# V ahead of the state-space scan in the first head block, the weights of one deferred segment mean asked for sooner, and two deferred means put later in stage 2

## The chip, the cores and the metric

The kernel runs on one core of a Trainium2 chip. The metric is the device time of one execution in microseconds (us). The kernel before takes 1317.5 us (median of 4 runs, 1315.62 to 1318.15). A program on one core has no other core to compare its clock with, so a run counts as slow only if it is more than 1.5% above the fastest of the same kernel.

Names of engines: PE is TensorE's matmul stream, DVE is VectorE, ACT is ScalarE, POOL is GpSimd, SP is SyncE, whose queue issues nearly all DMA transfers here (SPq in the trace). A *tag* (P, R, S, O; psP and so on in the trace) names a set of buffers for matmul results.

## The reference, cut to what matters

Two independent layers share one launch, and their outputs are laid side by side.

```python
# A: a diagonal state-space layer (S5), x is 2048 x 1024
Bu = einsum('bld,pd->blp', x, B_bar)
for t in range(L):
    h = Lam_bar * h + Bu[:, t]
y = 2 * einsum('blp,dp->bld', hs, C).real + x * Dskip

# B: attention with 8 memory rows, over segments of 32 tokens, 32 heads of 128
for s in range(64):
    h = concat(mem, x_segment)            # 8 + 32 rows
    q, k, v = h Wq, h Wk, h Wv
    o = softmax(mask(q k^T * scale)) v
    o = o Wo;  mem = o[:8];  out_s = o[8:]
```

The kernel does not walk B's 64 segments one after the other. It first guesses each segment's memory rows from the mean of the segment before (mean of x, times Wv, times Wo), does all segments in parallel, and checks the guess at the end. The *segment means* in this text are the products of these means of x with Wv, one for each of eight head blocks of four heads.

## The kernel before

The parts that matter are the first phase, in which A's scan and B's V share the engines, and its seam with the second phase (stage 2).

For each of 8 blocks of A's state (`pc`) and each of 4 token blocks (`tb`), `stage1` runs 16 matmuls on A's transposed x and hands the result to VectorE, which does the complex scan: about twenty operations for each token block. Between these, `v_x` runs 32 matmuls of V for the same token block of B, and ScalarE evicts them.

```python
    def v_x(self, hb, w):                        # V = x Wv, four 512-token groups
        for q in range(4):
            st = self.wl.tile([128, 4, 512], BF16, name="b_vst", bufs=2)
            for i in range(4):
                t = 4 * q + i
                p = k.ps("P")                    # 3 buffers
                for c in range(KC):
                    k.PE.matmul(p[:], self.xe[:, c, t * 128:(t + 1) * 128], w[:, c, :], ...)
                k.copy("s", st[:, i, :], p[:])   # ScalarE
                ...                              # store to DRAM after each group

    def og(self, hb, w):                         # one head block's segment means
        p = k.ps("R")                            # 1 buffer
        for h in range(4):
            for c in range(KC):
                k.PE.matmul(p[:, h * NSEG:(h + 1) * NSEG], w[:, c, h * 128:(h + 1) * 128], self.xbar[:, c, :], ...)
        k.V.tensor_copy(self.ogT[:, hb * 4:(hb + 1) * 4, :], p[...])
```

Before the means can be formed, VectorE must have summed x over each segment (`sum_x`, 18 reductions, most of 1.1 us here). It is done with that in block 2; the means of blocks 2 to 7 then follow inside the loop, and those of blocks 0 and 1 are *deferred* to stage 2, where their weights are loaded a second time:

```python
            a.load_x(0)
            b.load_x(0)
            ...
            for pc in range(PC):
                v = b.v_x(pc, wv)
                for tb in range(NB):
                    if pc == 0 and tb + 1 < NB:
                        a.load_x(tb + 1)
                    a.stage1(pc, tb)
                    if pc == 0:
                        b.load_x(tb + 1)
                    if tb == 1 and pc + 1 < PC:
                        nxt = b.load_wv(pc + 1)          # b_wv has two buffers
                    ...
                    for _ in range(4):
                        next(v, None)
                    if pc >= 1:
                        next(sx, None), next(sx, None)   # two sums over x
                if pc == 2:
                    b.fin_xbar(p1)
                if pc >= 2:
                    b.og(pc, wv)
        ...
            g = b.guess(p2)              # means times Wo, pieces of 2 MB (b_wog)
            s2 = a.stage2(p2)            # 32 halves of 16 matmuls each
            wv = [b.load_wv(0), b.load_wv(1)]
            for i, _ in enumerate(s2):
                if i in (1, 2):
                    b.og(i - 1, wv[i - 1])
                if i > 2 and i % 2 == 1:
                    next(g, None)
                if i == 16:
                    b.load_wqk(0)        # q and k weights of the next phase
```

Inside stage 2, each half ends with a VectorE addition into `a_ot` (two buffers), and each pair with a store of that tile. Stores, loads of the next x (`a_xn`), of the scan's states (`a_hl`) and of `b_wog` all go through the one queue of SP:

```python
                    V.tensor_tensor(ot[:, hs], py[:], xd[:, hs], ALU.add)
                    yield
                k.SP.dma_start(self.out[0, t0:t0 + 128, 0:D], ot[:])
                if 4 * tb + tt + 3 < TT:
                    load_xn(4 * tb + tt + 3, k.SP)
```

The order of instructions on each engine is set when the program is built, by a scheduling pass, and is not the order of the source. `keep_in_program_order` and `issue_after` are the builder's means to pin it.

## Time and profile before

| | before |
|---|---|
| time, median | 1317.5 us |
| span of the profiled run | 1314.3 us |
| PE busy | 1265.9 us (96%) |
| first large matmul | 14.53 us |
| first segment mean (end of the VectorE-bound part) | 148.30 us |
| stage 2 begins | 377.76 us |

The page of the kernel before, part 1 (busy time of each engine) and two rows of part 2 (busy tenths in 40 slices of the span, about 33 us each):

```profile
PE 1265.9 (96%) x7807; PEld 658.7 (50%) x7874; DVE 673.4 (51%) x1500; ACT 426.6 (32%) x1135; POOL 211.0 (16%) x291
PE   5999999999969999999999999999999989999997
DVE  6999998988821214555555555545555530001000
```

PE is the limit over the whole, with holes in the first slice and in the twelfth, which is the seam before stage 2. VectorE's 51% is an average: it is at 8 or 9 tenths in slices 2 to 11 and low afterwards. The windows view splits it at the first mean (columns: window, length, then busy time and instruction count of PE, PEld, DVE, ACT, POOL, granted clock, DMA share, GB/s):

```profile
18.00:148.30 130.30, 123.19 (x557) 55.08 (x566) 130.03 (x253) 48.51 (x85) 3.88 (x27) 1.00 0.76 185
148.30:361.00 212.70, 211.66 (x1130) 99.33 (x1149) 193.34 (x366) 75.39 (x134) 8.51 (x10) 1.00 0.40 123
```

Up to 148 us, VectorE is busy for 130.03 of 130.30 us and PE for only 123.19; from there on PE is busy for 211.66 of 212.70 us and VectorE for only 193.34.

The chain of waits of PE (what it waited for, total us, times, longest), then that of VectorE in the first 149 us:

```profile
PE psR L398 <- DMA b_wv<-in_B_Wv_dram: 8.1, 1, 8.1
PE psR L135 <- DMA a_r_119<-in_A_log_dt_dram: 6.8, 1, 6.8
PE psS L225 <- DMA a_xT<-in_A_x_dram: 6.6, 1, 6.6
PE psR L398 <- DVE b_ogT L399: 4.5, 1, 4.5
PE psP L380 <- ACT b_vst L62: 3.6, 6, 1.1
PE psP L380 <- DMA b_xe<-in_B_x_dram: 2.9, 2, 2.4
```

```profile
DVE b_xsum L353 <- DMA b_xe<-in_B_x_dram: 5.8, 1, 5.8
DVE a_raw L137 <- PE psR L135: 4.6, 1, 4.6
DVE ones L75 <- PEq L931: 0.9, 1, 0.9
```

L135 is the small transpose of A's parameters, from which VectorE makes the scan's tables. PE does nothing large before 14.5 us. VectorE idles 4.6 us for the parameters and 5.8 us for B's first x; these and two small waits sum to 11.5 us, and after 18 us it never stops.

The first large matmul and then the seam, in the timeline of PE (start, duration, instruction group, in brackets the idle time before and its releaser):

```profile
14.53 3.18 PE L225 MATMUL psS<-a_xT,a_bt_178 128*128 128x512 bf16 x8 [6.63 <-DMA a_xT<-in_A_x_dram]
...
360.17 1.10 PE L398 MATMUL psR<-b_xbar,b_wv 128*128 128x64 bf16 x32
365.73 1.87 PE L398 MATMUL psR<-b_xbar,b_wv 128*128 128x64 bf16 x32 [4.46 <-DVE b_ogT L399]
375.65 1.89 PE L398 MATMUL psR<-b_xbar,b_wv 128*128 128x64 bf16 x32 [8.06 <-DMA b_wv<-in_B_Wv_dram]
377.76 1.85 PE L289 MATMUL psO<-t_105,a_hl_3615 128*128 128x512 bf16 x5 [0.22 <-issue]
```

The mean of block 7 is followed by that of block 0, which waits until VectorE has copied block 7's out of the only buffer of tag R, then by that of block 1, which waits for its weights. Only then does stage 2 (L289) begin, although the source puts both means behind halves of stage 2. VectorE is late with that copy partly because one of its scans took 4.61 us at 355.99 us, where others take 1.28, while GpSimd ran two multiplications of 2.14 and 2.12 us from 355.30 on:

```profile
355.30 2.14 POOL L282 TENSOR_TENSOR a_xd<-a_xn_3609,a_dB 128x1024 f32<-128x1024 bf16 x1
...
355.99 4.61 DVE L237 TENSOR_TENSOR_SCAN a_wr<-a_rr,a_nx,a_wr 128x512 f32<-128x512 f32 x1
```

The Trainium skill, "SBUF — State Buffer", "SBUF: two separate sides", tells of a port pair for which a VectorE operation with two SBUF inputs and a GpSimd operation that reads SBUF exclude each other; this trace agrees at this one place, with 4.61 us for the scan.

The 8 matmuls at 14.53 take 3.18 us and a later group of 8 takes 1.89: a cold start. The Trainium skill, "TensorE: Matmul & The Clock Gate", Part 1, gives half the clock after an idle window of about 3.4 us; here the first matmuls after such a pause lie 0.43 us apart and later ones 0.216, which agrees.

### The profile page before, as it was taken

What the parts mean: (1) busy time and instruction counts of PE and PEld (TensorE: products, weight loads), DVE (VectorE), ACT (ScalarE), POOL (GpSimd) and SP (SyncE); (2) the same over time, 40 slices, a digit from 0 to 9 for tenths busy, and PEclk for the clock granted to TensorE, in tenths of its full rate; (3) what the DMA queues carried; (4) which work ended last, traced back from release to release, by engine and by line L of the source; (5) the groups of instructions that cost most, each with busy time, mean ns of one, the idle gap of its engine ahead of it and who ended that gap; (6) DMA issues with size and microseconds to landing.
All of it is one profiled execution on the core that took longest, in us unless ns stands there. A gap on an engine that the chain in (4) does not pass through costs nothing. (4 is left out here: it accounts for less than half of the span.)

```text
span 1314.3 us, 20077 instructions
## 1 busy us (share of the span) xinstructions
PE 1265.9 (96%) x7807; PEld 658.7 (50%) x7874; DVE 673.4 (51%) x1500; ACT 426.6 (32%) x1135; POOL 211.0 (16%) x291
## 2 busy tenths in 40 slices
PE   5999999999969999999999999999999989999997
PEld 2444444444435545555555555555555544444443
DVE  6999998988821214555555555545555530001000
ACT  3433333333200001554544454444545540001000
POOL 5000000000112221222222222222222220000000
PEclk9999999999979999999999999999999989999999
DMA  9983443344399519323343434333333470403000
GB/s 248 246 199 116 120 131 100 107 129 144 120 258 321 167 48 255 91 83 110 99 133 99 133 99 133 99 89 95 91 88 81 136 241 17 136 24 121 16 25 18
DMA packets 230843, 163.15 MB, mean 124 GB/s; under 512 B 74880, under 2 KB 214768, under 8 KB 230744
## 3 DMA queue, kind: packets, MB, share of 16 engines
q1 hardware_dynamic: 229272, 158.18, 42.1%
q0 software_dynamic: 1408, 3.61, 0.8%
q8 instruction: 63, 1.03, 0.3%
q14 instruction: 36, 0.29, 0.1%
q10 hardware_dynamic: 64, 0.02, 0.0%
HBM read 95.72 MB, written 49.30 MB: 110 GB/s over the span
## 5 line engine op out<-in xcount | busy, mean ns | idle before, releaser
L380 PE MATMUL psP<-b_wv,b_xe 128*128 128x512 bf16 x1021 | 227.4, 379 | 6.6 <-ACT b_vst L62 3.6
L516 ACT ACTIVATE b_e<-psS 99x396 bf16<-99x396 f32 x176 | 88.2, 501 | 417.9 <-PE psS L513 415.7
L519 POOL TENSOR_TENSOR b_m<-b_e,maskB 99x396 bf16<-99x396 bf16 x160 | 139.4, 871 | 351.6 <-ACT b_e L516 351.6
L539 DVE TENSOR_TENSOR b_ot<-psO,b_r 128x384 bf16<-128x384 f32 x176 | 98.1, 557 | 188.6 <-ACT b_r L533 169.8
L380 PEld LDWEIGHTS <-b_xe 128*128 128x128 bf16 x1024 | 99.9, 98 | 129.3 <-issue 5.9
L604 PEld LDWEIGHTS <-b_ol 128*128 128x128 bf16 x896 | 87.8, 98 | 106.5 <-issue 1.9
L64 DVE CAST b_ost<-psP 128x512 bf16<-128x512 f32 x16 | 11.1, 692 | 193.5 <-PE psP L604 193.5
L62 ACT ACTIVATE b_vst<-psP 128x512 bf16<-128x512 f32 x128 | 73.6, 586 | 109.5 <-PE psP L380 90.0
L604 PE MATMUL psP<-t_4702,b_ol 128*128 128x512 bf16 x438 | 99.7, 382 | 0.7 <-issue 0.2
L604 PE MATMUL psP<-wo_12093,b_ol 128*128 128x512 bf16 x438 | 98.8, 379 | 0.5
L533 ACT ACTIVATE b_r<-b_ln 128x396 f32<-128x396 f32 x176 | 94.0, 534 | 5.4
L532 ACT ACTIVATE b_ln<-psR 128x396 f32<-128x396 f32 x176 | 86.9, 494 | 0.0
L62 ACT ACTIVATE b_ost<-psP 128x512 bf16<-128x512 f32 x16 | 9.6, 597 | 211.4 <-PE psP L604 198.2
L291 DVE TENSOR_TENSOR a_ot<-psO,a_xd 128x512 bf16<-128x512 f32 x32 | 22.1, 692 | 94.9 <-PE psO L289 87.5
L64 DVE CAST b_k_4707<-psP 128x480 bf16<-128x480 f32 (+2 forms) x96 | 48.7, 529 | 30.6 <-PE psP L489 30.0
L528 PE MATMUL psR<-b_m,ones 99*128 99x396 bf16 x176 | 59.2, 337 | 3.1 <-POOL b_m L519 2.2
L537 PE MATMUL psO<-b_m,b_v 99*128 99x99 bf16 x704 | 61.5, 209 | 0.0
L64 DVE CAST b_k_4715<-psP 128x480 bf16<-128x480 f32 (+2 forms) x96 | 48.7, 528 | 21.3 <-PE psP L489 21.3
L64 DVE CAST b_q_4703<-psP 128x480 bf16<-128x480 f32 (+2 forms) x96 | 48.7, 528 | 17.5 <-PE psP L489 17.5
L537 PEld LDWEIGHTS <-b_v 99*128 99x128 bf16 x704 | 50.6, 98 | 13.3 <-DVE b_omT L542 0.6
L64 DVE CAST b_q_4711<-psP 128x480 bf16<-128x480 f32 (+2 forms) x96 | 48.6, 527 | 12.5 <-PE psP L489 12.5
L248 ACT ACTIVATE a_gr<-a_wr 128x512 bf16<-128x512 f32 x32 | 20.2, 630 | 68.7 <-DVE a_wr L237 68.7
(722 smaller groups left out, 1950.9 us busy)
## 6 DMA issues: line engine op xcount, KB each, us to landing
b_wv<-in_B_Wv_dram SPq DMA_DIRECT2D x16, 1024.0 KB
b_wog<-in_B_Wo_dram SPq DMA_DIRECT2D x4, 2048.0 KB
out_dram<-a_ot SPq DMA_DIRECT2D x16, 256.0 KB
t_4702<-in_B_Wo_dram SPq DMA_DIRECT2D x1, 4096.0 KB
b_ol<-b_os_90 SPq DMA_DIRECT2D x4, 1024.0 KB
b_ol<-b_os_91 SPq DMA_DIRECT2D x4, 1024.0 KB
b_ol<-b_os_92 SPq DMA_DIRECT2D x4, 1024.0 KB
wo_12093<-in_B_Wo_dram SPq DMA_DIRECT2D x1, 4096.0 KB
```

Of the source, the lines that this page charges most:

```text
L62: self.S.activation(out, in_, ACT.Copy)
L64: self.V.tensor_copy(out, in_)
L291: V.tensor_tensor(ot[:, hs], py[:], xd[:, hs], ALU.add)
L380: k.PE.matmul(p[:], self.xe[:, c, t * 128:(t + 1) * 128], w[:, c, :], start=(c == 0), stop=(c == KC - 1))
L516: k.S.activation(e[:], s[0:GW], ACT.Exp, scale=float(E) ** -0.5, accum_out=self.accE[0:GW, i:i + 1])
L519: k.G.tensor_tensor(m[:], e[:], mask[0:GW, :, :].unsqueeze(2).to_broadcast([GW, 2, 2, GW]), ALU.mult)
L528: PE.matmul(sm[:, 0:W4], k.ones[0:GW, :], mf, start=True, stop=True)
L532: k.S.activation(ln[:], sm[:, 0:W4], ACT.Ln)
L533: k.S.activation(r[:].rearrange("p a b q -> p (a b q)"), ln[:], ACT.Exp, scale=-1.0, accum_out=self.accR[:, i:i + 1])
L537: PE.matmul(o[:, gg, hh, :], vt[:, 2 * u + gg, hh * 128:(hh + 1) * 128], m[:, gg, hh, :], start=True, stop=True)
L539: V.tensor_tensor(ot[:, :, 2 * u * GX:(2 * u + 2) * GX].rearrange("p h (g n) -> p g h n", n=GX), o[:, :, :, 0:GX], r[:, :, :, 0:GX], ALU.mult)
L604: PE.matmul(p[:], lhs, self.wo[half][:, h, :], start=(h == 0), stop=(h == H - 1))
```

## The change

The intent has two parts. *Start*: V needs only B's x and Wv, so in head block 0 V of each 512 tokens is put ahead of the scan of its token block, and B's first x comes in four pieces of 128 tokens, so that PE can start at the first of them. *Middle*: the weights of block 0's deferred mean are fetched at `pc == 7` instead of at the seam, and both means are moved behind the third and fifth half of stage 2, into tag P, which has three buffers.

```diff
     def load_x(self, q):
+        for t, c, n in self.chunks(q):
+            step = 128 if q == 0 else n
+            for o in range(0, n, step):
+                self.k.SP.dma_start_transpose(self.xe[:, :, c + o:c + o + step], self.x[0][t + o:t + o + step, :])
 ... (chunks of 512, 512, 512, 384 and twice 64 tokens in place of four of 480 and twice 64)
-    def og(self, hb, w):
-        p = k.ps("R")
+    def og(self, hb, w, tag="R"):
+        p = k.ps(tag)
 ...
             wv = b.load_wv(0)
-            b.wl.tile([128, 4, 512], BF16, name="b_vst", bufs=2)
+            b.load_x(0)
             a.params(p1, p1)
 ...
             a.load_x(0)
-            b.load_x(0)
 ...
-                    if pc == 0 and tb + 1 < NB:
-                        a.load_x(tb + 1)
+                    if pc == 0:
+                        for _ in range(4):
+                            next(v, None)
+                        if tb + 1 < NB:
+                            b.load_x(tb + 1)
+                            a.load_x(tb + 1)
                     a.stage1(pc, tb)
-                    if pc == 0:
-                        b.load_x(tb + 1)
-                    if tb == 1 and pc + 1 < PC:
-                        nxt = b.load_wv(pc + 1)
+                    if tb == 1:
+                        nxt = b.load_wv((pc + 1) % PC)
 ...
-                    for _ in range(4):
-                        next(v, None)
+                    if pc > 0:
+                        for _ in range(4):
+                            next(v, None)
 ...
-            wv = [b.load_wv(0), b.load_wv(1)]
+            wv = [wv, b.load_wv(1)]
             for i, _ in enumerate(s2):
-                if i in (1, 2):
-                    b.og(i - 1, wv[i - 1])
-                if i > 2 and i % 2 == 1:
+                if i in (2, 4):
+                    b.og(i // 2 - 1, wv[i // 2 - 1], "P")
+                if i > 4 and i % 2 == 1:
                     next(g, None)
```

More of the change, by code (lines that the diff above doesn't have):

```diff
@@ L337, in load_x, with chunks @@
     def load_x(self, q):
-        k = self.k
-        if q < 4:
-            parts = [(64 + 480 * q, 480 * q, 480)]
-        else:
-            parts = [(0, XMAIN, 64), (T - 64, T - 64, 64)]
-        for t, c, n in parts:
-            k.SP.dma_start_transpose(self.xe[:, :, c:c + n], self.x[0][t:t + n, :])
+        for t, c, n in self.chunks(q):
+            step = 128 if q == 0 else n
+            for o in range(0, n, step):
+                self.k.SP.dma_start_transpose(self.xe[:, :, c + o:c + o + step], self.x[0][t + o:t + o + step, :])
+    @staticmethod
+    def chunks(q):
+        if q < 3:
+            return [(64 + 512 * q, 512 * q, 512)]
+        return [(64 + 1536, 1536, 384), (0, XMAIN, 64), (T - 64, T - 64, 64)]
     def sum_x(self):
         k = self.k
-        for t, c, n in [(64 + 480 * q, 480 * q, 480) for q in range(4)] + [(0, XMAIN, 64), (T - 64, T - 64, 64)]:
+        for t, c, n in sum((self.chunks(q) for q in range(4)), []):
             m = 2 if n > 64 else KC
```

## The prediction

> **What bounds the kernel now.** TensorE (PE): 1265.9 of 1314.3 us busy (page, part 1); some 48 us are idle: 14.5 until its first large matmul; 2.9 for pieces of B's x and 3.6 for ScalarE's evictions of psP, up to 148 us; and between the last scan block and stage 2 (361 to 377 us) 4.5 for VectorE's copy of the previous segment mean (one buffer of tag R), then 8.1 for the weights of head block 1 (chain of waits, timeline). After such pauses the first six or seven matmuls are 0.43 us apart, later ones 0.216: the half clock of the Trainium skill, "TensorE: Matmul & The Clock Gate", Part 1 (some 3.4 us after idling); this trace agrees with about 3 us, a loss of about 1.5 us each time.
>
> VectorE (DVE) is the second limit: from 18.0 to 148 us it is busy 129.7 of 130.0 us (windows), and PE's waits for evictions come from it. Before that it idles 5.8 us, until B's first x lands at 18.0.
>
> **What the change does.** PE's work is the same.
>
> 1. Start. B's x comes first, in 128-token pieces. A 512-token transpose takes about 4.5 us of the queue, so a piece should take 1.1 to 1.3. The DMA share is above 1 from 0 to 80 us at about 250 GB/s. From the trace's landing times (1.25 MB by 8.0 us, 2.5 MB by 14.5, then about 0.26 MB per us) I estimate: Wv and the first piece at 8 us, A's first x at 18 to 19. PE starts at 8, runs 32 V matmuls (about 8.5 us with the cold start), waits 2 us, and scans from 18.5 instead of 14.5. VectorE's first product comes no sooner, but its former idle time takes the first sums over x (1.2 us each) and parameters. So of PE's 6.5 us VectorE allows its idle 5.8 less some delay: I expect 3 to 6 us left at 148 us, kept afterwards since PE binds from there (101.5 of 102 us busy to 250).
>
> 2. Middle. The source moves the means behind the third and fifth half of stage 2, into tag P. If they run there, waits of 12.7 us and a cold restart of about 2 us go: about 14 us, less some DMA pressure (share 1.07 from 370 to 430 us). But an engine's order is not the source's: before, too, the source put both means behind stage-2 halves, and the trace has both ahead of the first. Nor is the fetch sooner: block 0's weights were already issued at 321 us, and block 1's (367 us) still wait for the last mean to free their buffer. If both means are again hoisted, PE waits for the same landing at 375.6 us, and nothing is gained. I give hoisting 0.65.
>
> **Sum.** Hoisted: about 1312. Not hoisted: about 1298. I say 1309 us, range 1296 to 1317. Faster by over 2% (below 1291) needs more than both gains: 0.04; within 2%: 0.95; slower: 0.01.
>
> **What would show it.** Timeline of PE: first large matmul (L380) near 8 us, first L225 at 18 to 19; VectorE's idle time before 18 us mostly gone; the first mean (148.3 us before) 3 to 6 us earlier. Middle: whether L289 follows the mean of block 7 directly or after two more, and whether the wait of 8 us for b_wv is gone or has grown to about 13.
>
> **What would make it wrong.** Pieces of x or stores queued between them hold up A's x by over 5 us, so the start becomes a loss; stage 2, begun sooner, outruns its loads; or the means are not hoisted and the start gives 6 us or more (1295).

## The result, and the profile after

The kernel after takes 1314.55 us (median of 4 runs, 1313.92 to 1316.48) against 1317.5 us. Ratios in this text are the mean time of one kernel's fast runs over that of the other's of the same rounds, so they are not quite the ratios of the medians quoted. Here the ratio is 0.9982, with a 95% interval of 0.9965 to 1.0. That is about 2.4 us (0.18% of 1317) and at the edge of what the runs can tell from nothing. The prediction was 1309 us, a gain of 8.5 us, more than three times as much.

The page after, part 1, and the waits of PE:

```profile
PE 1267.0 (97%) x7808; PEld 658.2 (50%) x7874; DVE 673.7 (51%) x1500; ACT 427.1 (33%) x1135; POOL 211.4 (16%) x291
```

```profile
PE psP L383 <- DMA b_xe<-in_B_x_dram: 11.2, 4, 8.0
PE psP L401 <- DMA b_wv<-in_B_Wv_dram: 10.0, 1, 10.0
PE psP L383 <- ACT b_vst L62: 4.7, 6, 2.9
```

The waits for A's parameters and for `b_ogT` are gone from PE's list, and the wait for `b_wv` has grown from 8.1 to 10.0 us.

*The start did what was intended, on PE.* PE's timeline after:

```profile
8.02 1.89 PE L383 MATMUL psP<-b_wv,b_xe 128*128 128x512 bf16 x4 [8.02 <-DMA b_xe<-in_B_x_dram]
9.85 0.20 PE L135 MATMUL psR<-ident,a_r_122 24*128 24x24 bf16 x1
...
19.88 1.89 PE L225 MATMUL psS<-a_xT,a_bt_181 128*128 128x512 bf16 x8 [2.27 <-DMA a_xT<-in_A_x_dram]
...
146.68 1.89 PE L383 MATMUL psP<-b_wv,b_xe 128*128 128x512 bf16 x8 [2.88 <-ACT b_vst L62]
148.40 1.10 PE L401 MATMUL psR<-b_xbar,b_wv 128*128 128x64 bf16 x32
```

The first large matmul begins at 8.02 us instead of 14.53. At the first mean all of that is gone: 148.40 us against 148.30. PE had the V products done sooner, and then waited longer. The wait of 2.88 us at 146.68 shows for what. It names ScalarE, which was to evict the V product; ScalarE's own timeline shows that it stood at another instruction, one that needed VectorE (the second line is the eviction that PE waited for):

```profile
145.42 0.72 ACT L193 ACTIVATE a_tabc_1760<-a_k_1764,hpb 128x513 f32<-128x513 f32 x1 [3.56 <-DVE a_wi L232]
146.05 0.58 ACT L62 ACTIVATE b_vst<-psP 128x512 bf16<-128x512 f32 x1
```

So the limit up to 148 us is VectorE's list of work, and what counts is VectorE's idle time before it. Its waits after, up to 149 us:

```profile
DVE a_raw L137 <- PE psR L135: 7.6, 1, 7.6
DVE b_xsum L356 <- DMA b_xe<-in_B_x_dram: 1.7, 2, 1.2
DVE a_wr L229 <- PE psS L225: 1.1, 2, 0.9
DVE ones L75 <- PEq L936: 0.9, 1, 0.9
```

The wait for B's x fell from 5.8 to 1.7 us, as intended. But the parameters' transpose (L135) now stands behind four V matmuls, which start only when x has landed at 8.02 us, so the wait for it rose from 4.6 to 7.6; and 1.1 us of waits for the scan's own input came in, because A's x now lands at 19.88 us instead of 14.53. With one more of 0.2 the total is 11.5 us, the same as before.

*The middle.* PE's timeline at the seam:

```profile
360.26 1.10 PE L401 MATMUL psR<-b_xbar,b_wv 128*128 128x64 bf16 x32
361.90 1.09 PE L401 MATMUL psP<-b_xbar,b_wv 128*128 128x64 bf16 x32 [0.54 <-ACT b_vst L62]
372.99 1.89 PE L401 MATMUL psP<-b_xbar,b_wv 128*128 128x64 bf16 x32 [9.99 <-DMA b_wv<-in_B_Wv_dram]
374.69 0.61 PE L289 MATMUL psO<-t_105,a_hl_3617 128*128 128x512 bf16 x1
```

Both means were hoisted ahead of stage 2's first half again. Tag P removed the wait of 4.5 us before block 0's mean, and the wait for block 1's weights took it over. They landed 2.66 us sooner (372.99 against 375.65), though their load was issued at the same moment (367.07 against 366.98 us, SP's timeline). That is about the whole of the gain; what may be behind it stands under e12.

### The profile page after: what moved, and what is told of

It is laid out like the page before. It is cut to its first block, busy times and chain, and to the rows that moved or that the text cites. A ratio compares the mean times of both kernels' runs of the same rounds, so it can differ in the third digit from the quotient of the medians.

```text
span 1312.2 us, 20083 instructions
## 1 busy us (share of the span) xinstructions
PE 1267.0 (97%) x7808; PEld 658.2 (50%) x7874; DVE 673.7 (51%) x1500; ACT 427.1 (33%) x1135; POOL 211.4 (16%) x291
## 5 line engine op out<-in xcount | busy, mean ns | idle before, releaser
L383 PE MATMUL psP<-b_wv,b_xe 128*128 128x512 bf16 x1024 | 229.8, 381 | 16.0 <-DMA b_xe<-in_B_x_dram 11.2
L383 PEld LDWEIGHTS <-b_xe 128*128 128x128 bf16 x1024 | 100.0, 98 | 139.3 <-DMA b_xe<-in_B_x_dram 12.7
```

## The experiments

Twelve kernels ran; a thirteenth did not build (see e8). The questions, in plain words; the expectations use letters of their own for the theories.

- For the start: is it worth nothing because VectorE's total idle time is fixed by when data arrive; or because the parameters were pushed behind V (which an order could mend); or is the early PE start worth something that another part of the change took back?
- For the middle: is the intended gain lost because the builder hoisted the means; or would stage 2, started sooner, run into a new wait; and which?

"End of stage 2" below is the start of the first `v_mem` matmul in the profiled run: 496.57 us before, 494.59 after. "Before" had medians of 1316.86 us (11 runs) beside the first four kernels, 1317.65 (9) beside the next four and 1317.73 (9) beside the last four. Each ratio is to the kernel before of the same rounds.

### e1_start_only: the start alone

```diff
 (the kernel after, with the middle of the kernel before)
-                    if tb == 1:
-                        nxt = b.load_wv((pc + 1) % PC)
+                    if tb == 1 and pc + 1 < PC:
+                        nxt = b.load_wv(pc + 1)
-            wv = [wv, b.load_wv(1)]
+            wv = [b.load_wv(0), b.load_wv(1)]
 ... (means behind the halves of before, in tag R)
```

> The kernel before with only the new start (B's x first in 128-token pieces, V of a token block ahead of its scan block). Theory T1 (VectorE decides when the first segment mean runs, and its total idle time up to there is the same, 11.5 us in both kernels): first mean (L401) at 148.4 us as in the kernel after, total within 1 us of the kernel before (1316.5 to 1318.5). Rival T2 (the new start does gain 3 to 6 us and the middle gives it back): total 1312 to 1315.

Measured: 1317.96 us (5 runs), ratio 0.9999 (0.9982 to 1.0016). The first mean came at 150.64 us. VectorE's waits up to there were 7.7 + 1.6 + 1.3 + 0.9 + 0.8 + 0.6 = 12.9 us. T1 had said 148.4 and 11.5, so both came out higher; by how much such figures scatter from kernel to kernel is worked out in the last part. The time is as T1 had it: the new start alone is worth nothing that can be seen.

### e2_middle_only: the middle alone

```diff
 (the kernel before, with the middle of the kernel after: load_wv((pc + 1) % PC),
  both means in tag P behind the third and fifth half)
```

> The kernel before with only the new middle (deferred means in tag P, later in the source, head block 0's weights requested in the last scan round). Theory T1: the whole gain of the kernel after is here: both means still run before the first half of stage 2, the weights of head block 1 land 2.7 us sooner because one 2 MB load instead of two is queued behind them; total 2 to 3 us below the kernel before (1314.5 to 1315.5). Rival T2: no gain or a loss here (1317 or more).

Measured: 1315.26 us (6 runs), ratio 0.9987 (0.9969 to 1.0004). The wait for block 1's weights was 9.8 us, issue to use 5.7 us, end of stage 2 at 495.70. If the change gains anything, it gains it here: this kernel's ratio cannot be told from that of the whole change (0.9982).

### e3_means_pinned: the means where the source has them

```diff
-                k.PE.matmul(p[:, h * NSEG:(h + 1) * NSEG], w[:, c, h * 128:(h + 1) * 128], ...)
+                mm = k.PE.matmul(p[:, h * NSEG:(h + 1) * NSEG], w[:, c, h * 128:(h + 1) * 128], ...)
+                if tag == "P":
+                    k.tc.keep_in_program_order(mm)
```

> The kernel after, with the first matmul of each deferred mean tied in issue order behind the stage-2 half that precedes it in the source. Theory M1 (the gain was lost because the builder put both means first on TensorE, so that it waits for weights): the wait of 10.0 us for b_wv and the cold restart go, stage 2 starts at about 361.5 us instead of 374.7, total 11 to 13 us below the kernel after (1302 to 1304). Rival M2 (stage 2 is held by its transfers, DMA share 1.07 there): the wait turns into waits for a_hl or b_wog, and less than 4 us is gained (1311 or more).

Measured: 1311.48 us (6 runs), ratio 0.9952 (0.9935 to 0.9968), so about 4 us below the change (0.9952 against 0.9982), where 11 to 13 had been expected. The trace shows both halves of the answer. The wait for `b_wv` is gone and stage 2 begins at 362.88 us instead of 374.69. But a new wait stands 23 us later. PE's waits, VectorE's timeline and SP's timeline of this kernel:

```profile
PE psS L416 <- DVE b_ogT L404: 5.7, 1, 5.7
```

```profile
390.37 0.69 DVE L291 TENSOR_TENSOR a_ot<-psO,a_xd 128x512 bf16<-128x512 f32 x1 [11.86 <-DMA out_dram<-a_ot]
390.98 0.41 DVE L404 CAST b_ogT<-psP 128x256 bf16<-128x256 f32 x1
```

```profile
370.05 8.33 SPq L277 DMA_DIRECT2D a_hl<-a_hs  x2
...
380.38 0.38 SPq L293 DMA_DIRECT2D out_dram<-a_ot  x1
```

The guess (L416) needs VectorE's copy of block 1's mean. VectorE stands 11.86 us at an addition whose `a_ot` buffer is still being stored; the store of the first output tile, whose last addition started at 369.98 us, was issued only at 380.38, behind two loads of `a_hl` at which SP's queue stood 8.33 us, and took some 10 us to land. So hoisting did cost something; but a stage 2 that begins sooner also outran its queue.

### e4_params_first: the parameters ahead of V

```diff
-        PE.matmul(pr[:, 0:3 * PC], r24[:], ...)
+        self.pm = PE.matmul(pr[:, 0:3 * PC], r24[:], ...)
 ...
+                        if tb == 0:
+                            with tc.issue_after(a.pm.ins):
+                                next(v, None)
```

> The kernel after, with the first V matmul tied in issue order behind the small parameter matmul (L135). Theory T1 (VectorE's idle time decides): L135 runs at 6.8 us instead of 9.85, VectorE's wait for it falls from 7.6 to 4.6 us, the first mean comes 2 to 3 us sooner (145.5 to 146.5 instead of 148.4), total 2 to 3 us below the kernel after (about 1312). Rival T3 (after the start, the landing of A's x at 19.9 us decides, VectorE only idles elsewhere instead): first mean and total within 0.7 us of the kernel after.

Measured: 1315.40 us (6 runs), ratio 0.9981 (0.9962 to 0.9999): the same as the change. L135 ran at 6.89 us, and VectorE's wait for it went back to 4.6. Its other wait grew in return:

```profile
DVE b_xsum L356 <- DMA b_xe<-in_B_x_dram: 6.5, 2, 3.9
DVE a_raw L137 <- PE psR L135: 4.6, 1, 4.6
DVE ones L75 <- PEq L939: 0.9, 1, 0.9
```

The sum is 12.0 us against 11.5. The order of the parameters is not the cause; with them done sooner, VectorE stands at the next thing that x's arrival decides.

### e5_dve_plus and e6_dve_plus_late: 4.8 us more of VectorE's work, early and late

Four needless sums of 1.2 us were pinned into block 1 (e5), or into block 4, after the first mean (e6). The result is still the right one.

```diff
+                    if pc == 1:                  # e6: pc == 4
+                        xtra = p1.tile([128, 32], FP32, name="x_extra", bufs=1)
+                        tc.keep_in_program_order(k.V.tensor_reduce(xtra[:], b.xe[:, 0:2, 0:512].rearrange(...), AX.X, ALU.add))
```

> The kernel after with four needless sums of 1.2 us each added on VectorE in the second head block (about 64 to 105 us), result correct. Theory T1 (VectorE's total of work and idle time up to the first segment mean decides when TensorE reaches it): first mean about 4.9 us later (153 to 154 us instead of 148.4 to 149.5), total 4 to 5 us above the kernel after (1318 to 1319.5). Rival T3 (transfers of x hold TensorE, VectorE has room): under 1 us later.

> The same four sums in the fifth head block (190 to 230 us), where VectorE idles about 5.6 us in 102. Theory T1: no later than the kernel after by more than 1 us, as TensorE alone binds there. If VectorE's work counts everywhere: 4 to 5 us later, as in the run with the sums early.

Measured, early: 1319.98 us (5 runs), ratio 1.0015 (1.0001 to 1.0029), about 4.3 us above the change for 4.8 us of work (1.0015 - 0.9982 = 0.33% of 1317). Late: 1314.76 us (5 runs), ratio 0.9978 (0.9965 to 0.9992): free. The two were timed in the same rounds, and their runs do not overlap (1317.53 to 1321.10 early, 1314.08 to 1315.95 late). The sums overlap a little with their neighbours: by the page VectorE's busy time grew by 4.1 us early (677.8 against 673.7) and 3.7 late (677.4). The early one's cost did not appear in the place that had been expected. The first mean came at 150.09 us, only 1.7 later than after. In this kernel the mean itself waited for VectorE, after V was done:

```profile
150.09 1.89 PE L401 MATMUL psR<-b_xbar,b_wv 128*128 128x64 bf16 x32 [4.02 <-DVE b_xbar L366]
...
152.20 3.19 PE L225 MATMUL psS<-a_xT,a_bt 128*128 128x512 bf16 x7 [0.22 <-issue]
```

The pause made PE cold: the mean took 1.89 us instead of 1.10, and the next seven matmuls 3.19 instead of 1.89. That is most of the rest, and the last mean of the loop comes at 364.61 us, 4.35 later than after.

### e7_dve_minus: 3.9 us less of VectorE's work, early

```diff
-                        a.tables(pc + 1)
+                        if pc > 0:
+                            a.tables(pc + 1)
```

Block 1 uses block 0's tables, so A's result is not the right computation. (The comparison with the reference did not notice it.)

> The kernel after without the tables of the second head block (it reuses those of the first, so part A's result is wrong on purpose; B is unaffected); takes about 3.9 us of VectorE and 2.7 us of ScalarE away before 105 us. Theory T1: first mean 3 to 4 us sooner (144.5 to 146 us), total 3 to 4 us below the kernel after. Rival T3 (transfers of x): under 1 us sooner.

Measured: 1312.83 us (5 runs), ratio 0.9960 (0.9946 to 0.9974), about 2.9 us below the change; first mean at 146.36 us, 2.0 sooner, both a little short of what T1 expected. By the page VectorE's busy time fell by 2.8 us (670.9 against 673.7), not 3.9. The runs (1310.28 to 1313.95) lie below all those of e6 in the same rounds. ScalarE also lost work here (2.3 us by the page), but e5 and e6 changed VectorE alone. Together the three show, from both sides, that VectorE's work before the first mean sets the time and its work after it does not.

### e8_pin_store_act: pinned means, output stores on ScalarE's queue

```diff
 (e3, and)
-                k.SP.dma_start(self.out[0, t0:t0 + 128, 0:D], ot[:])
+                k.S.dma_start(self.out[0, t0:t0 + 128, 0:D], ot[:])
```

> The pinned kernel (e3) with stage 2's output stores issued by ScalarE, which is idle there, instead of the queue that also carries the loads. In e3 the store of the first output tile was issued at 380.4 us and landed at 390.4, VectorE waited 11.9 us for it and TensorE 5.7 us. Theory M3 (the store stood in order behind loads that the queue could not issue): the store goes out near 371 us, TensorE's wait of 5.7 us and its cold restart go, total 6 to 8 us below e3 (1304 to 1306). Rival M2 (the DMA engines are full there, share 1.10): the wait moves to other tiles, total within 2 us of e3.

Measured: 1307.92 us (5 runs), ratio 0.9920 (0.9906 to 0.9934), about 4 us below e3, between what M3 (6 to 8) and M2 (within 2) had said. The wait of 5.7 us has gone; smaller ones are left:

```profile
PE psS L416 <- DMA b_wog<-in_B_Wo_dram: 2.9, 1, 2.9
...
PE psO L289 <- DVE a_ot L291: 1.4, 1, 1.4
```

So the store's going through SP's queue was the cause of e3's wait. SP's queue stood as long at the two loads as before (8.28 us), but the first store went out on ScalarE's queue at 374.54 us instead of 380.38, and the addition that needs its buffer ran at 381.56 instead of 390.37. The store thus also landed faster, in about 7 us instead of 10; how much each of the two was worth is not separated. Not all waiting for stores went: VectorE's came to 22.5 us in stage 2, after 30.1 in e3. (The other way to free that addition, four buffers of `a_ot`, did not fit: 89.16 kB for each partition were needed where 87.81 were left, so it never ran.) With the wait out of the way, the 2 MB pieces of Wo come late by a little; the DMA share (mean busy share of the DMA engines) between 380 and 420 us was 1.11.

### e9_mid_pin_store: the same with the start of before

```diff
 (e2, with the edits of e3 and e8)
```

> The kernel of e8 (pinned means, output stores by ScalarE) with the start of the kernel before. Theory T1 (the new start is worth nothing): total within 2 us of e8, which was 0.992 of the kernel before, and the first mean near 148 to 149.5 us. Rival (the new start is worth its 3 to 6 us once the middle no longer hides it): 3 us or more slower than e8, ratio 0.9945 or above.

Measured: 1307.57 us (5 runs), ratio 0.9922 (0.9908 to 0.9936); the first mean came at 148.73 us. Nothing tells it from e8. The new start is worth nothing with a mended middle either.

### e10_wqk_late: the next phase's weights out of the way

```diff
 (e8, and the loads of q and k weights that stage 2 starts are kept in the source's order,
  so that they come behind stage 2's own first transfers)
-                self.k.SP.dma_start(w[:], self.Wf[i][:, :, hp * 256:(hp + 1) * 256])
+                d = self.k.SP.dma_start(w[:], self.Wf[i][:, :, hp * 256:(hp + 1) * 256])
+                if late:
+                    self.k.tc.keep_in_program_order(d)
```

> The kernel of e8 with the 2 MB of q and k weights (needed only near 490 us) kept in source order behind stage 2's own transfers. Theory M2 (in e8 what is left in stage 2 is transfer volume: TensorE waits 4.3 us there, DMA share 1.11): those waits shrink to about 1 us, total 2 to 4 us below e8 (ratio about 0.9895). Rival (order, not volume): no change against e8.

Measured: 1302.43 us (4 runs), ratio 0.9887 (0.9872 to 0.9902). This is the fastest kernel, about 15 us below the kernel before (1.13% of 1317) and 12 below the change (0.9982 - 0.9887 = 0.95%). Against e8 it is about 4 us by the ratios (0.9920 - 0.9887), at the upper end of what was expected. PE's waits in stage 2 are gone from its list, and its timeline shows the first deferred mean between the halves without a pause (the second, at 378.85 us, has none either):

```profile
360.65 10.52 PE L289 MATMUL psO<-t,a_hl 128*128 128x512 bf16 x47
371.01 1.10 PE L401 MATMUL psP<-b_xbar,b_wv 128*128 128x64 bf16 x32
```

### e11_one_piece: the first x in one transfer

```diff
-            step = 128 if q == 0 else n
+            step = n
```

> The kernel after with the first 512 tokens of B's x in one transfer instead of four pieces. Theory T1 (when TensorE starts does not matter, VectorE binds): the first V matmul about 3 us later (11 to 12 us instead of 8.0), VectorE's idle time within 1 us of 11.5, first mean and total within 1 us of the kernel after. Rival (the start of TensorE counts): 3 us later.

Measured: 1315.72 us (5 runs), ratio 0.9984 (0.9970 to 0.9998). The first V matmul moved from 8.02 to 12.35 us, the first mean of this profile from 148.40 to 150.02, and the time by nothing that can be told from noise. VectorE's waits up to there came to 5.5 + 4.8 + 0.9 + 0.9 + 0.6 = 12.7 us; this and the first mean lie a little outside the 1 us that T1 had allowed, but inside the scatter given in the last part. PE's start, in itself, is not on the critical path.

### e12_wog_one_buffer: why do block 1's weights land sooner?

In the kernel before, two pieces of 2 MB of `b_wog` are issued behind block 1's weights; in the kernel after, one, and then loads of `a_hl`. The suspicion was that the second piece slows the weights. So the kernel before was given one buffer of `b_wog`.

```diff
-            wo = pool.tile([128, H, 256], BF16, name="b_wog", bufs=2)
+            wo = pool.tile([128, H, 256], BF16, name="b_wog", bufs=1)
```

> The kernel before with one buffer instead of two for the 2 MB pieces of Wo, so that only one of them is queued behind the weights of head block 1. Theory (the second piece queued behind them slows these weights): from issue to TensorE's first use 5.9 us as in the kernel after instead of 8.7 in the kernel before; TensorE's wait for b_wv falls from 8.1 us to about 5.5; the total may still rise since the second piece now comes too late for its own user. Rival: no change of that wait.

Measured: 1326.71 us (4 runs), ratio 1.0074 (1.0058 to 1.0090); this kernel waits 6.3 us more for later pieces, as a single buffer must. The weights took 7.5 us from issue to use (368.53 to 376.05), where 5.9 was expected, and PE's wait for them was 7.0 us, not 5.5. With two pieces behind them they took 8.7 (before) and 6.8 (e1); with one, 5.9 (after), 5.7 (e2) and 7.5 (here). The ranges overlap: the number of pieces does not explain it.

The packets in the traces point elsewhere. In the three kernels with slow weights (before, e1, e12) a packet of 16384 bytes on the queue that the page lists as `instruction` (q8) starts 0.14 to 0.17 us after the weights' load is issued. In the other eleven of the fourteen kernels it starts 3.6 to 5.1 us before that issue. And of the sixteen packets of 4 bytes that come as the load ends, all sixteen are through 5.1 to 5.4 us after the issue in those eleven, while in the three only fifteen are through by 5.5 us and the last comes at 7.9, 6.2 and 6.9 us. So one part of the load was late, and a fetch of instructions beside it is the likely cause. It is not shown: all three also have the old middle, and no run moved the fetch alone.

## Why the prediction was right or wrong, point by point

**What bounds the kernel: right.** VectorE up to the first mean, PE after it. Work added to VectorE early cost about 4.3 us for 4.1 us more of its busy time (e5), work taken away gained about 2.9 for 2.8 less (e7), work added late cost nothing (e6).

**Where PE and the loads would stand: nearly right, but for the pieces.** The first matmul came at 8.02 us (8 predicted), the first L225 at 19.88 (18 to 19 predicted). The four pieces took 7.38 us of the queue together, 1.85 each, where 1.1 to 1.3 had been worked out by dividing a 512-token transfer by four. The trace of before held a better guide: its two transposes of 128 rows at the same place in the queue (A's B matrices, from 1.34 us on) took 2.14 and 2.49 us.

**"I expect 3 to 6 us left at 148 us": wrong; 0 was left.** This is the step of the start that failed, and within it the term "VectorE allows its idle 5.8 less some delay". The prediction took the one wait that the change attacks, 5.8 us on B's x, as time to be gained. It even saw that "VectorE's first product comes no sooner", and then counted on sums over x and parameters to fill the hole. The sums did: four of them ran between 11.75 and 17.75 us. But the parameters moved back by 3.0 us, with L135 behind V's matmuls, and the scan's input by 5.35. VectorE's idle time before the first mean was 11.5 us in both kernels. One profile of each could mislead, as the first mean scatters by over 1 us; but over the four kernels with the old start (before, e2, e9, e12) it came at 148.30 to 149.61 us, 149.04 in the mean, and over the six with the new start and VectorE's early work unchanged (after, e1, e3, e6, e8, e10) at 147.85 to 150.64, again 149.04 in the mean. The idle times were 11.5 to 12.6 and 11.2 to 12.9 us. Putting L135 first moved the idle time onto x (e4), so it is not one bad order. Fetching x whole cost nothing (e11), and the start of before did as well as the new one in three pairs: the change without it (e2 and after), the kernel before with it (e1), and the mended middle (e8 and e9). That the arrival of both x's sets this idle time fits all of these; no run made x arrive sooner, so that much is argued and not shown.

**Both means hoisted: right, as the more likely of two cases.** The trace shows both ahead of L289, as before.

**"PE waits for the same landing at 375.6 us, and nothing is gained": off by 2.7 us.** The weights landed at 372.99, and that is the small gain that there is. Nothing in the prediction led to it, so this gain is luck; its likely cause, an instruction fetch that fell at another moment, is not shown (e12).

**"About 14 us, less some DMA pressure", if the means are not hoisted: mis-sized.** This was given a weight of 0.35, so 14 times 0.35, or 4.9 us, of the forecast gain came from it, and the rest from the start. The case did not occur, and when it was brought about (e3) it gave 4 us below the change, since stage 2, begun sooner, ran into a wait of 5.7 us for a store behind loads in SP's queue, and further smaller ones, where the prediction had set down "some DMA pressure". With the stores on another queue (e8) and the next phase's weights later (e10), 12 us came out. The estimate of the waits was sound; what was not costed is that stage 2 begun 12 us sooner needs its buffers and loads 12 us sooner too, which the prediction had named among the risks.

## What to carry to other kernels

When an engine is saturated, a change gains only by what it takes out of that engine's *total* idle time and work up to the point where the limit changes: sum all its waits before and after, for a wait that shrinks may come back as another of the same length. The order of the source is not the order of the engine, so read where an instruction ran before you count on moving it, and pin it if the place is the point of the change. A stage that begins sooner also asks sooner for its buffers and transfers: look at what stands before each store and load in its queue, and cost that with the gain.

## What the Trainium skill lacked or had wrong

- "DMA: Bandwidth & Descriptors", "Issuing engines are not separate DMA queues", says that issuing from several engines saves only the sequencer's time to initiate, "usually small relative to the DMA itself". Here it was not small: SP's queue stood 8.33 us at two `a_hl` loads with a 256 KB store behind them (e3), and moving the stores to ScalarE's queue removed a PE wait of 5.7 us and about 4 us of the time (e8 against e3). The page could add that a transfer held up in a queue holds up those behind it.
- "DMA: Bandwidth & Descriptors" has a count of cycles for a transposing instruction with small tiles, in a part on trn3; no page was found that gives the queue time of a transposing transfer of 128 rows on this chip. Here the first transposes of 128 rows took 1.85 us (mean of four) to 2.49 us each, and the same size later 1.35 and 1.37 (the kernel after, at 8.76 and 10.18 us), against about 4.5 for 512 tokens.
- "TensorE: Matmul & The Clock Gate", Part 1, puts the cold ramp for modelling at under 1% of a typical span. That holds for the span here too, but not for a change of this size: in e5 a pause of 4.02 us cost 2.1 us more by the ramp (0.79 on a group of 32 small matmuls, 1.30 on the next seven large ones), as much as the whole change gained (about 2.4 us).
- No page was found on what a fetch of instructions does to a load that is issued at the same moment. Block 1's weights, 1 MB, took 6.8 to 8.7 us from issue to use in the three kernels where such a packet of 16384 bytes started within 0.2 us of the issue, and 5.7 to 5.9 in two where it had come before (e12); that it is the cause is not shown.
